# Side work in a routed expert kernel re-spaced: counts one turn behind comparisons, every turn used, a free turn between weight conversions, late pieces from the first network on

## The chip, the cores and the metric

The kernel runs on one core of a Trainium2 chip. Its engines are TensorE (PE, with PEld for the weight loads that overlap it), VectorE (DVE), ScalarE (ACT), GpSimd (POOL) and SyncE (SP, which issues most transfers). The metric is device time in microseconds (us), median of three runs; lower is better.

## The reference, cut to what matters

Three stages follow each other: a gated linear attention over 768 steps, a routed network with eight experts that each take exactly 384 of the 3072 tokens, and one dense network with a cosine in it that every token passes. The routed order is greedy: the logits of all tokens and experts are sorted, and each token goes to the first expert that still has room.

```python
for idx in order:                       # logits, largest first
    tok, e = (int(idx) // E, int(idx) % E)
    if assigned[tok] >= 0 or counts[e] >= cap:
        continue
    assigned[tok] = e
    counts[e] += 1
...
for e in range(E):
    mask = assigned == e
    h = np.maximum(x[mask] @ w1[e], 0.0)
    out[mask] = h @ w2[e]
...
h = x @ w_in
g = h * np.cos(h)
return (g @ w_out).astype(np.float32)
```

Here x has 384 columns, w1 is 384 x 1024, w2 1024 x 384, w_in 384 x 2048 and w_out 2048 x 384. w_in and w_out arrive as 64-bit floats and are brought to 32 bits on the chip.

## The kernel before, in words

Every product is made as three matmuls on a high and a low part of each operand (`mm3`), so one 128 x 384 tile of result with K = 384 costs nine matmuls of 384 columns. The greedy routing is turned into eight rounds: each round fills the expert that saturates first. While the tokens of one expert pass both networks (a stage of `experts`, n = 0 to 7), the routing of the next one runs beside it as side work.

The main work of a stage: a transpose of the gathered tokens (`xpose`, tile xtp, 9 small matmuls), the first network in eight steps `up` (tile pA) and `down` (accB), then the second network in sixteen steps `up2` (pC) and `down2` (accD), where `down2` runs three steps behind `up2`. Each of these is nine matmuls; a piece of nine is called a turn below. `up2` and `finish` also make the cosine: ACT ki (L785), DVE ki (L787), ACT sine (L790), DVE product (L792), ACT gh (L800) and POOL gl (L801); `down2` needs gh and gl.

The side work of a stage is a generator, `beside`. It runs `route` for the next expert, and inside it `search`: six steps k, each of which compares the tokens' best logits with up to 64 thresholds on DVE (tile C, L549, in two halves), counts on PE (tile cn, L545, 12 or 6 small matmuls), forms sat on DVE, sums over thresholds on PE (num, L572) and makes the next thresholds on DVE (thr, L589 or L597). `route` then ranks tokens (rk, L632), compares (L, L661) and inverts the ranks (xi, L658) to the list of tokens (idx). After that `prefetch` gathers those tokens (xg, three indirect transfers that POOL issues) and starts the fetch of weights (raw, from SP), and five calls of `convert` split the weights (ACT wh L723, POOL wl L724).

A second generator, `convert_late`, brings the last six pieces of w_out to 32 bits in stage 0: ACT L137, DVE L139 and L140, DVE L142 and L143, then ACT woh L146 and POOL wol L147; a piece is four calls of `next(late, None)`.

What decides the place of the side work is `tick`, called 42 times in a stage: after each `up` and `down`, and after each `up2` and `down2` but a few. Before the change it advances the side work two times out of three. ACT keeps the written order; PE, DVE and POOL are put in order by a scheduler when the program is built, which keeps close to the written order.

Of the kernel before, what the change touches and what calls it, by code (L numbers as in the profile page):

```python
# [525 lines left out]
def search(nc, K, rp, ps, Z, n, em, found):  # L526
    V, PE = nc.vector, nc.tensor
    mx, oh = Z["mx"], Z["oh"]
    steps = FIRST if n == 0 else LATER
    thr, tau, old = K["t0"].bitcast(F32)[:, ::2 ** (steps[0] - 25)], None, None  # L530
    for k, st in enumerate(steps):
        T = 2 ** ((32 if k == 0 else steps[k - 1]) - st)
        g = P // T if n > 0 else 1
        if st:
            nx = steps[k + 1]
            wd = 2 ** (st - nx)
        if k == 0 and n == 0:
            cn = Z["cn"]
        else:
            C = rp.tile([P, NU, T], BF16, name="C", tag="C")  # L540
            cn = ps.tile([g * T, g * E], F32, name="cn", tag="rt")

            def count(a, z):
                for c in range(a, z, g):
                    PE.matmul(cn, C[:, c:c + g].rearrange("p c t -> p (c t)"), oh[:, c:c + g].rearrange("p c e -> p (c e)"), start=(c == 0), stop=(c == NU - g))  # L545

            cuts = (0, 15, NU) if n == 0 else tuple(range(0, NU + 1, HALF))
            for a, z in zip(cuts, cuts[1:]):
                V.tensor_tensor(C[:, a:z], mx[:, a:z, None].to_broadcast([P, z - a, T]), thr[:, None, :].to_broadcast([P, z - a, T]), op=ALU.is_ge)  # L549
                if n == 0:  # L550
                    count(a, z)
            if n > 0:
                count(0, NU)
            if st and k:
                base = rp.tile([P, wd], I32, name="base", tag="base")
                V.scalar_tensor_tensor(base, K["io"][:, :wd], nx, tau.to_broadcast([P, wd]), op0=ALU.logical_shift_left, op1=ALU.bitwise_xor)
            yield
        sat = rp.tile([T, E], BF16, name="sat", tag="sat")
        if g == 1:
            V.tensor_scalar(sat, cn, CAP - 0.5, None, op0=ALU.is_ge)  # L560
        else:
            less = None
            for j in range(1, g):
                part = cn[j * T:(j + 1) * T, j * E:(j + 1) * E]
                more, less = less, rp.tile([T, E], F32, name="less", tag="less", bufs=2)
                if j == 1:
                    V.tensor_scalar(less, part, -1.0, None, op0=ALU.mult)
                else:
                    V.scalar_tensor_tensor(less, part, -1.0, more, op0=ALU.mult, op1=ALU.add)
            V.scalar_tensor_tensor(sat, cn[:T, :E], 0.5 - CAP, less, op0=ALU.add, op1=ALU.is_ge)  # L570
        num = ps.tile([P, E], F32, name="num", tag="rt")
        PE.matmul(num, K["onesb" if st == 0 else "ones0"][:T], sat, start=True, stop=True)  # L572
        ix = rp.tile([P, 1], I32, name="ix", tag="ix")
        if st == 0:
            top = rp.tile([P, 1], F32, name="top", tag="top")
            V.tensor_reduce(top, num, axis=AX, op=ALU.max)
            sel = rp.tile([P, E], F32, name="sel", tag="sel")
            V.scalar_tensor_tensor(sel, num, top, K["eb"], op0=ALU.is_equal, op1=ALU.mult)
            V.tensor_reduce(em, sel, axis=AX, op=ALU.max)
            V.tensor_scalar(ix, top, -1.0, None, op0=ALU.add)  # L580
            V.tensor_tensor(found, ix, tau, op=ALU.bitwise_xor)
            yield
            break
        with nc.allow_low_precision(reason="small whole numbers"):
            V.tensor_reduce(ix, num, axis=AX, op=ALU.max)
        old, tau = tau, rp.tile([P, 1], I32, name="tau", tag="tau", bufs=2)
        if k:
            thr = rp.tile([P, wd], I32, name="thr", tag="thr", bufs=2)
            V.scalar_tensor_tensor(thr, ix.to_broadcast([P, wd]), st, base, op0=ALU.logical_shift_left, op1=ALU.bitwise_xor)  # L589
            V.scalar_tensor_tensor(tau, ix, st, old, op0=ALU.logical_shift_left, op1=ALU.bitwise_xor)  # L590
        else:
            t2 = rp.tile([P, 1], I32, name="t2", tag="t2i")
            V.tensor_scalar(tau, ix, st, -2**31, op0=ALU.logical_shift_left, op1=ALU.bitwise_xor)
            V.tensor_scalar(t2, tau, 31, 0x7FFFFFFF, op0=ALU.arith_shift_right, op1=ALU.bitwise_and)
            V.tensor_tensor(tau, tau, t2, op=ALU.bitwise_xor)
            thr = rp.tile([P, wd], I32, name="thr", tag="thr", bufs=2)
            V.scalar_tensor_tensor(thr, K["io"][:, :wd], nx, tau.to_broadcast([P, wd]), op0=ALU.logical_shift_left, op1=ALU.bitwise_xor)  # L597
        thr = thr.bitcast(F32)
        yield
    if n == 0:  # L600
        V.tensor_copy(Z["ems"], em)
    else:
        V.tensor_tensor(Z["ems"], Z["ems"], em, op=ALU.add)
# [84 lines left out]
def experts(tc, nc, ctx, K, R, Z, xs, wcat, wout, out):  # L688
# [29 lines left out]
    def convert(r, f, eng=None):  # L718
        if f < NA:
            raw = r["raw"].pop(f)  # L720
            h = mp.tile([P, 2 * HD], F32R, name="wh", tag="wh", bufs=5)
            l = mp.tile([P, 2 * HD], F32R, name="wl", tag="wl", bufs=5)
            SC.copy(h, raw)  # L723
            (eng or GP).tensor_tensor(l, raw, h.bitcast(F32), op=ALU.subtract)  # L724
            r["w"][f] = (h, l)
            fetch(r, f + 3)
# [30 lines left out]
    def up(r, f):  # L757
        p = mmp.tile([P, HD], F32, name="pA", tag="mm")
        wh, wl = r["w"][f]
        for k in range(3):  # L760
            s = slice(k * P, (k + 1) * P)
            mm3(p, (wh[:, s], wl[:, s]), r["xT"][k], k == 0, k == 2)
        r["h"][f] = split(p, "h", 3, "h", relu=True)
# [66 lines left out]
    late = convert_late(nc, mp, R, wout)  # L830
# [17 lines left out]
    with in_order(tc, nc, (mybir.EngineType.Activation,)):  # L848
        for n in range(E):
            r = cur  # L850
            nxt = second if n == 0 else fresh() if n < E - 1 else None

            def beside():
                if nxt is not None:
                    if n == 0:
                        next(steps)
                        hold(tc, nc, mybir.EngineType.DVE, mark)
                        yield
                    yield from steps if n == 0 else route(nc, K, rp, rtp, Z, n + 1, nxt)
                    prefetch(nxt)  # L860
                    yield
                    for f in range(5):
                        convert(nxt, f)
                        yield
            side = beside()
            count = [0]

            def tick():
                count[0] += 1
                if count[0] % 3:  # L870
                    next(side, None)
            for f in range(2, NA):
                up(r, f)
                tick()
                down(r, f - 2)
                convert(r, f + 3)
                tick()
            for d in range(3):
                down(r, NA - 2, (d,))
                down(r, NA - 1, (d,))  # L880
            tick()
            for f in range(LEAD):
                up2(r, f, (0, 1))
            for f in range(LEAD):
                up2(r, f, (2,))
            for f in range(LEAD, LAG):
                up2(r, f)
                next(late, None)
                tick()
                next(late, None)  # L890
            down2(r, (0,))
            tick()
            for f in range(LAG, NF):
                up2(r, f)
                next(late, None)
                tick()
                down2(r, (f - LAG + 1,))
                next(late, None)
                tick()
            for f in range(NF + 1 - LAG, NF - 2):  # L900
                down2(r, (f,))
                tick()
            for _ in side:
                pass
            if nxt is not None:
                xpose(nxt)
                down2(r, (NF - 2,))
                up(nxt, 0)
                up(nxt, 1)
                down2(r, (NF - 1,))  # L910
            else:
                down2(r, (NF - 2, NF - 1))
            cur = nxt
# [95 lines left out]
```

## Time and profile before

| | |
|---|---|
| median of 3 runs | 872.75 us (871.38 to 873.23) |
| profiled execution, its own time | 871.95 us |
| its span, first to last instruction | 870.2 us |
| mean granted TensorE clock | 0.976 |
| stage 0, from its first matmul at 201.13 to 291.74 us | 90.61 us |
| a stage with a search beside it (n = 1 to 5) | 82.73 to 83.26 us |
| the stage with routing but no search (n = 6) | 77.06 us |

The profiled execution lies 1.75 us above its span, and 0.8 us under the median. PE is busy for almost the whole of a stage, so a stage is as long as its matmuls and the holes between them.

### The profile page before, as it was taken

To read this page: it belongs to the slowest core of one execution; us is meant where nothing else is said; L and a number is where in the kernel's file an instruction comes from. 1 tells how busy PE (TensorE), PEld (TensorE's weight loads), DVE (VectorE), ACT (ScalarE), POOL (GpSimd) and SP (SyncE) were. 2 spreads that over 40 slices of the span, in tenths; PEclk is the share of its full clock that TensorE was granted. 3 is DMA by queue.
4 is the path that set the end of the run, shared out by engine and by line. 5 is a ranking of instruction groups with operands and counts; after the bars stand their busy time and mean duration, and the time that the engine had idled before them with its cause. 6 is when DMAs were issued, how large, how long until landed. Compare 5 with 4: busy or idle time off the path is not lost.

```text
span 870.2 us, 15619 instructions
## 1 busy us (share of the span) xinstructions
PE 810.0 (93%) x5886; PEld 760.0 (87%) x5886; DVE 529.8 (61%) x1365; ACT 423.8 (49%) x814; POOL 378.8 (44%) x329
## 2 busy tenths in 40 slices
PE   6989999648998899999999999999999999999996
PEld 4878889527988889999998999899989999999996
DVE  5888888565697368546844683567357645432332
ACT  4777776113355425632563356245624553753552
POOL 5545555013146513751384138314732563734233
PEclk9999999859999999999999999999999999999999
DMA  9988884142032201220131014002300133300000
GB/s 243 262 229 222 232 223 120 40 126 86 1 109 82 83 1 55 72 75 2 55 101 46 1 55 119 28 1 73 101 28 27 60 113 85 92 1 28 1 2 28
DMA packets 27348, 71.91 MB, mean 83 GB/s; under 512 B 4608, under 2 KB 7936, under 8 KB 27264
## 3 DMA queue, kind: packets, MB, share of 16 engines
q1 hardware_dynamic: 24192, 61.38, 24.7%
q0 software_dynamic: 3072, 9.44, 3.4%
q8 instruction: 49, 0.80, 0.4%
q14 instruction: 35, 0.29, 0.1%
HBM read 61.37 MB, written 9.44 MB: 81 GB/s over the span
## 4 chain that ended last, share of the span: by engine, by line
PE 47%; DVE 2%; ACT 1%; issue 0%; POOL 0%; POOLq 0%; ACTq 0%
PE accD L812 5%; PE accD L811 5%; PE accD L813 5%; PE pC L742 5%; PE pC L741 5%; PE pC L743 5%; PE accB L741 2%; PE pA L741 2%; PE accB L742 2%; PE accB L743 2%; PE pA L743 2%; PE pA L742 2%; DVE C L549 1%; DVE thr L597 1%; PE xtp L753 1%; PE cn L545 1%
## 5 line engine op out<-in xcount | busy, mean ns | idle before, releaser
L801 POOL TENSOR_TENSOR gl<-ki,gh 128x384 fp32r<-128x384 f32 x128 | 132.1, 1036 | 249.8 <-ACT gh L800 228.1
L813 PE MATMUL accD<-woh,gl 128*128 128x384 f32 x384 | 131.1, 341 | 5.6 <-POOL gl L801 5.6
L724 POOL TENSOR_TENSOR wl<-raw,wh 128x768 fp32r<-128x768 f32 x61 | 112.7, 1853 | 51.4 <-ACT wh L723 43.5
L811 PE MATMUL accD<-woh,gh 128*128 128x384 f32 x384 | 131.7, 343 | 0.5 <-ACT gh L800 0.5
L812 PE MATMUL accD<-wol,gh 128*128 128x384 f32 x384 | 130.9, 341 | 0.0
L743 PE MATMUL pC<-yTh,wil 128*128 128x384 f32 x384 | 130.3, 339 | 0.0
L741 PE MATMUL pC<-yTh,wih 128*128 128x384 f32 x384 | 130.0, 341 | 0.0
L742 PE MATMUL pC<-yTl,wih 128*128 128x384 f32 x384 | 129.9, 338 | 0.0
L787 DVE SCALAR_TENSOR_TENSOR ki<-pC,ki 128x384 f32<-128x384 f32 x128 | 71.0, 555 | 85.2 <-ACT ki L785 85.0
L785 ACT ACTIVATE ki<-pC,quarter 128x384 int32<-128x384 f32 x128 | 73.7, 576 | 92.2 <-PE pC L743 90.9
L792 DVE TENSOR_TENSOR ki<-pC,ki 128x384 f32<-128x384 f32 x128 | 71.0, 555 | 53.8 <-ACT ki L790 50.3
L790 ACT ACTIVATE ki<-ki,halfpi 128x384 f32<-128x384 f32 x128 | 79.0, 617 | 43.9 <-DVE ki L787 43.6
L732 ACT ACTIVATE hh<-pA 128x384 fp32r<-128x384 f32 x64 | 31.5, 492 | 114.9 <-PE pA L743 114.9
L723 ACT CAST wh<-raw 128x768 fp32r<-128x768 f32 x64 | 52.3, 828 | 61.6 <-PE accB L742 32.2
L813 PEld LDWEIGHTS accD<-woh,gl 128*128 128x128 f32 x384 | 72.7, 189 | 7.3 <-POOL gl L801 7.2
L733 DVE SCALAR_TENSOR_TENSOR hl<-pA,hh 128x384 fp32r<-128x384 f32 x64 | 35.5, 555 | 63.1 <-ACT hh L732 62.9
L811 PEld LDWEIGHTS accD<-woh,gh 128*128 128x128 f32 x384 | 72.8, 189 | 0.9 <-ACT gh L800 0.8
L742 PEld LDWEIGHTS pC<-yTl,wih 128*128 128x128 f32 x384 | 72.5, 189 | 0.6 <-DVE yTl L736 0.5
L800 ACT CAST gh<-ki 128x384 fp32r<-128x384 f32 x128 | 64.8, 506 | 16.8 <-DVE ki L792 16.6
L812 PEld LDWEIGHTS accD<-wol,gh 128*128 128x128 f32 x384 | 72.6, 189 | 0.0
L741 PEld LDWEIGHTS pC<-yTh,wih 128*128 128x128 f32 x384 | 72.5, 189 | 0.1
L743 PEld LDWEIGHTS pC<-yTh,wil 128*128 128x128 f32 x384 | 72.5, 189 | 0.0
(187 smaller groups left out, 1688.8 us busy)
## 6 DMA issues: line engine op xcount, KB each, us to landing
raw<-in_wcat_dram SPq DMA_DIRECT2D x64, 384.0 KB, 3.4
ring<-in_qk_dram SPq DMA_DIRECT2D x48, 192.0 KB, 5.0
vf<-in_qkvf_dram SPq DMA_DIRECT2D x23, 384.0 KB, 4.9
wr<-in_win_dram SPq DMA_DIRECT2D x12, 512.0 KB, 5.4
xs<-xx SPq DMA_DIRECT2D x24, 192.0 KB, 2.7
wr<-in_wout_dram SPq DMA_DIRECT2D x10, 384.0 KB, 4.8
lr<-in_wout_dram SPq DMA_DIRECT2D x6, 384.0 KB, 3.3
vf<-in_qkvf_dram SPq DMA_DIRECT2D x2, 192.0 KB, 3.2
```

Of the source, the lines that this page charges most:

```text
L724: (eng or GP).tensor_tensor(l, raw, h.bitcast(F32), op=ALU.subtract)
L741: PE.matmul(o, ah, bh, start=first, stop=False)
L742: PE.matmul(o, ah, bl, start=False, stop=False)
L743: PE.matmul(o, al, bh, start=False, stop=last)
L785: SC.activation(ki, p, AF.Identity, bias=quarter, scale=INV2PI)
L787: V.scalar_tensor_tensor(fr, p, INV2PI, ki, op0=ALU.mult, op1=ALU.subtract)
L790: SC.activation(fr, fr, AF.Sin, bias=halfpi, scale=TWO_PI)
L792: V.tensor_tensor(g, p, fr, op=ALU.mult)
L801: GP.tensor_tensor(gl, g, gh.bitcast(F32), op=ALU.subtract)
L811: PE.matmul(r["accD"][t], gh[:, s], R["oh"][:, f], start=(f == 0), stop=False)
L812: PE.matmul(r["accD"][t], gh[:, s], R["ol"][:, f], start=False, stop=False)
L813: PE.matmul(r["accD"][t], gl[:, s], R["oh"][:, f], start=False, stop=(f == NF - 1))
```

## The change

It moves the counts of a search (n > 0) one step of the side work behind the comparisons, lets every turn advance the side work, puts an empty step behind each of the five weight conversions, and calls the late pieces twice per step of the first network in stage 0 and once per step of the second (before: only in the second, twice per step).

```diff
@@ -550,6 +550,7 @@
                 if n == 0:
                     count(a, z)
             if n > 0:
+                yield
                 count(0, NU)
             if st and k:
                 base = rp.tile([P, wd], I32, name="base", tag="base")
@@ -862,18 +863,18 @@
                     for f in range(5):
                         convert(nxt, f)
                         yield
+                        yield
             side = beside()
-            count = [0]
 
             def tick():
-                count[0] += 1
-                if count[0] % 3:
-                    next(side, None)
+                next(side, None)
             for f in range(2, NA):
                 up(r, f)
+                next(late, None)
                 tick()
                 down(r, f - 2)
                 convert(r, f + 3)
+                next(late, None)
                 tick()
             for d in range(3):
                 down(r, NA - 2, (d,))
@@ -887,7 +888,6 @@
                 up2(r, f)
                 next(late, None)
                 tick()
-                next(late, None)
             down2(r, (0,))
             tick()
             for f in range(LAG, NF):
@@ -895,7 +895,6 @@
                 next(late, None)
                 tick()
                 down2(r, (f - LAG + 1,))
-                next(late, None)
                 tick()
             for f in range(NF + 1 - LAG, NF - 2):
                 down2(r, (f,))
```

In steps of the side work: a stage with a search had 20 steps of `route`, one of `prefetch` and five of `convert`, spread over turns 1 to 38; it now has 26, 1 and 10, over turns 1 to 37. A comparison and the num of its step stay at the turns where they were (3k + 2 and 3k + 4); the count goes from turn 3k + 2 to 3k + 3. `prefetch` goes from turn 31 to 27, and the conversions from 32, 34, 35, 37, 38 to 28, 30, 32, 34, 36. Stage 0 is one turn ahead of that.

On PE, the second search step of a middle stage (num is the sum of the step before, accB_5760 the first of the three results of `down`, cn the counts). Before:

```order
L743 MATMUL pA<-xTh,wl 128x384
L741 MATMUL accB_5760<-hh,wh 128x384
L742 MATMUL accB_5760<-hl,wh 128x384
L743 MATMUL accB_5760<-hh,wl 128x384
L545 LDWEIGHTS C
L545 MATMUL cn<-oh,C 128x16
```

With the change, a few rows further on in the same `down`:

```order
L742 MATMUL accB_5762<-hh,wh 128x384
L743 MATMUL accB_5762<-hl,wh 128x384
L744 MATMUL accB_5762<-hh,wl 128x384
L545 LDWEIGHTS C
L545 MATMUL cn<-oh,C 128x16
```

The first six counts stood after three of the nine matmuls of `down`, and the other six after four more; now all twelve stand together behind the nine. Third and sixth step, whose six counts stood in two threes, have them together too.

On DVE, the first search step of stage 0 (xTl belongs to the transpose, hl to `up`, lv and lr to the late pieces). Before:

```order
L736 TENSOR_TENSOR xTl<-xtp,xTh 128x384 x3
L549 TENSOR_TENSOR C<-mx,t_118 128x768 x2
L733 SCALAR_TENSOR_TENSOR hl<-pA,hh 128x384 x2
L567 TENSOR_SCALAR less<-cn 64x8
L570 SCALAR_TENSOR_TENSOR sat<-cn,less 64x8
L733 SCALAR_TENSOR_TENSOR hl<-pA,hh 128x384
L585 TENSOR_REDUCE ix<-num 128x1
```

With the change:

```order
L734 SCALAR_TENSOR_TENSOR hl<-pA,hh 128x384 x3
L139 TENSOR_SCALAR lv<-lv 128x384
L140 TENSOR_SCALAR lv<-lv 128x384
L142 SCALAR_TENSOR_TENSOR lv<-lr,lv 128x384
L568 TENSOR_SCALAR less<-cn 64x8
L143 SCALAR_TENSOR_TENSOR lv<-lr,lv 128x384
L571 SCALAR_TENSOR_TENSOR sat<-cn,less 64x8
L586 TENSOR_REDUCE ix<-num 128x1
```

All four operations of a late piece now stand ahead of sat, for which num waits.

On POOL, the end of stage 0 (wl are the conversions, wol the late pieces). Before:

```order
L706 DMA xg<-xs,idx 128x384 x3
L147 TENSOR_TENSOR wol<-lv,woh 128x384
L801 TENSOR_TENSOR gl<-ki,gh 128x384 x2
L147 TENSOR_TENSOR wol<-lv,woh 128x384
L724 TENSOR_TENSOR wl<-raw,wh 128x768
L801 TENSOR_TENSOR gl<-ki,gh 128x384
L724 TENSOR_TENSOR wl<-raw,wh 128x768
L801 TENSOR_TENSOR gl<-ki,gh 128x384
L724 TENSOR_TENSOR wl<-raw,wh 128x768
L147 TENSOR_TENSOR wol<-lv,woh 128x384
L724 TENSOR_TENSOR wl<-raw,wh 128x768
L801 TENSOR_TENSOR gl<-ki,gh 128x384
```

With the change:

```order
L707 DMA xg<-xs,idx 128x384 x2
L802 TENSOR_TENSOR gl<-ki,gh 128x384
L707 DMA xg<-xs,idx 128x384
L147 TENSOR_TENSOR wol<-lv,woh 128x384
L725 TENSOR_TENSOR wl<-raw,wh 128x768
L802 TENSOR_TENSOR gl<-ki,gh 128x384
L725 TENSOR_TENSOR wl<-raw,wh 128x768
L802 TENSOR_TENSOR gl<-ki,gh 128x384
L725 TENSOR_TENSOR wl<-raw,wh 128x768
L802 TENSOR_TENSOR gl<-ki,gh 128x384
L725 TENSOR_TENSOR wl<-raw,wh 128x768
L802 TENSOR_TENSOR gl<-ki,gh 128x384
```

One wl and one gl now alternate, one late piece less stands among them, and the gathers come two gl earlier. In the middle stages the gathers likewise go from behind nine gl to behind seven.

## Rows read from the trace of the kernel before

**Rows 1.** Stages: busy us (x instructions) of each engine, clock, DMA.
```profile
core 0: us, PE busy (x) PEld busy (x) DVE busy (x) ACT busy (x) POOL busy (x), PEclk, DMA share, GB/s
201.13:291.74 90.61, 82.65 (x492) 77.28 (x491) 65.74 (x163) 43.39 (x81) 40.76 (x34) 0.96 0.22 66
...
540.95:623.92 82.97, 81.50 (x513) 77.59 (x511) 50.32 (x140) 38.70 (x71) 36.71 (x31) 1.00 0.17 53
...
706.65:783.71 77.06, 77.06 (x458) 76.44 (x457) 33.35 (x67) 38.55 (x71) 36.88 (x31) 1.00 0.21 62
```

**Rows 2.** What PE waited for in stage 0: us, times, longest.
```profile
PE accD L813 <- POOL gl L801: 5.3, 3, 2.8
PE cn L545 <- DVE C L549: 0.8, 2, 0.6
PE rk L632 <- DVE R L630: 0.6, 1, 0.6
PE accD L811 <- ACT gh L800: 0.5, 1, 0.5
PE xi L658 <- DVE L L661: 0.4, 2, 0.3
PE num L572 <- DVE sat L570: 0.3, 1, 0.3
```

**Rows 3.** The same for the middle stage 540.95 to 623.92.
```profile
PE cn L545 <- DVE C L549: 1.3, 1, 1.3
```

**Rows 4.** Two stretches of the end of stage 0, columns as in Rows 1.
```profile
276.20:279.60 3.40, 3.40 (x12) 3.40 (x12) 3.37 (x4) 0.21 (x1) 2.27 (x2) 0.51 0.52 163
286.90:290.80 3.90, 3.90 (x16) 3.90 (x16) 1.11 (x2) 1.60 (x4) 3.90 (x4) 0.63 0.53 166
```

**Rows 5.** Timeline of PE, that stage's second search step.
```profile
554.11 0.18 PE L572 MATMUL num<-sat,ones 64*128 64x8 bf16 x1
...
557.91 0.31 PE L545 MATMUL cn<-oh,C 128*128 128x16 bf16 x6 [1.32 <-DVE C L549]
...
559.03 0.42 PE L742 MATMUL accB<-hl,wh 128*128 128x384 f32 x1
```

**Rows 6.** Timeline of PE, second search step of stage 0.
```profile
207.84 0.18 PE L572 MATMUL num<-sat,ones 64*128 64x8 bf16 x1
...
211.65 0.31 PE L545 MATMUL cn<-oh,C 128*128 128x16 bf16 x6 [0.29 <-DVE C L549]
212.52 0.31 PE L545 MATMUL cn<-oh,C 128*128 128x16 bf16 x6 [0.56 <-DVE C L549]
212.69 0.43 PE L741 MATMUL pA<-xTh,wh 128*128 128x384 f32 x1
```

**Rows 7.** Timeline of PE around the third and fourth counts, middle stage.
```profile
562.77 0.34 PE L743 MATMUL accB<-hh,wl 128*128 128x384 f32 x1
...
564.21 0.34 PE L742 MATMUL pA<-xTl,wh 128*128 128x384 f32 x1
...
568.39 0.34 PE L743 MATMUL pA<-xTh,wl 128*128 128x384 f32 x1
...
568.99 0.33 PE L742 MATMUL accB<-hl,wh 128*128 128x384 f32 x1
```

**Rows 8.** Timeline of DVE: third step's sat, sixth step's second comparison.
```profile
564.73 0.15 DVE L570 SCALAR_TENSOR_TENSOR sat<-cn,less 32x8 bf16<-32x8 f32 x1
...
583.30 0.54 DVE L549 TENSOR_TENSOR C<-mx,thr 128x384 bf16<-128x384 f32 x1
```

**Rows 9.** Timelines of POOL and DVE, end of stage 0.
```profile
275.45 1.94 POOL L724 TENSOR_TENSOR wl<-raw,wh 128x768 fp32r<-128x768 f32 x1
...
275.74 1.87 DVE L140 TENSOR_SCALAR lv<-lv 128x384 int32<-128x384 int32 x1
```

**Rows 10.** Timeline of POOL, gathers of the middle stage.
```profile
604.80 0.98 POOL L706 DMA_INDIRECT xg<-xs,idx  x1 [1.79 <-DVE idx L675]
606.09 0.96 POOL L706 DMA_INDIRECT xg<-xs,idx  x1 [0.30 <-PE accD L813]
607.07 1.02 POOL L801 TENSOR_TENSOR gl<-ki,gh 128x384 fp32r<-128x384 f32 x1
```

**Rows 11.** Tile thr: duration in ns, least, median, most.
```profile
L597 DVE SCALAR_TENSOR_TENSOR thr<-io,tau x7: 193/1769/1775, 168.1 to 638.1; 128x64 int32<-128x64 int32 x6, 128x32 int32<-128x32 int32 x1
```

**Rows 12.** Timeline of PE, the wait ahead of the first low clock.
```profile
275.55 0.44 PE L813 MATMUL accD<-woh,gl 128*128 128x384 f32 x1 [1.61 <-POOL gl L801]
```

## The prediction

> **What bounds the kernel now.** Read the stages first. In the middle stages PE is busy for 81.5 of 83 us, and a stage whose routing has no search takes 77.06 us [rows 1]; its 458 matmuls stand 0.17 us apart (77.06 / 458), nearly all of them large ones. So the main work sets the time, and all that the change can win is what the side work costs PE: some 6 us in each of the five stages n = 1 to 5, and in stage 0, which takes 90.61 us, more. Then read what PE waits for. In stage 0 the reader is to see waits for gl and gh of 5.3 + 0.5 = 5.8 us, and 0.8 + 0.6 + 0.4 + 0.3 = 2.1 us for the search and the ranks [rows 2]. In a middle stage it is one wait of 1.3 us for a comparison [rows 3]. [...] Last, the timelines show what a count costs where it doesn't wait. The attention and the first search, before 201 us, and the last stage have none of the changed code and stay.
>
> **The middle stages.** No count is added or removed; the gain is in waits and in seams between large and small matmuls.
>
> Second step. From num to the first large matmul behind the counts it takes 559.03 - 554.11 = 4.92 us, with 16 large matmuls in between [rows 5]; the wait is 1.32 us of that. The order puts 18 in between now, as stage 0 has them already: there it takes 212.69 - 207.84 = 4.85 us, and the two halves of the comparison are still waited for, 0.29 and 0.56 us [rows 6]. The comparison starts from the same num, so it ends no earlier, and two large matmuls more ahead of the counts do not cover it. I therefore take stage 0's figure: 4.92 - (4.85 - 2 x 0.17) = 0.4 us. Bounds: 0, and what it would be with no wait left. Stage 0's 4.85 less its two waits and 18 x 0.17 leaves 0.9 us for num and the counts themselves, so that is 4.92 - 16 x 0.17 - 0.9 = 1.3 us.
>
> Third step. Two groups of three counts with five large matmuls take 564.21 - 562.77 = 1.44 us, of which 1.44 - 5 x 0.17 = 0.6 is theirs; six in one group take 568.99 - 568.39 less 2 x 0.17 = 0.26 [rows 7]. Joined: 0.3 us. The sixth step is joined likewise, but its comparison's second half ends at 583.84 [rows 8], about where the joined group now stands, so I take 0.2 of that 0.3.
>
> The new order also shortens something: sat must be ready one turn (nine matmuls, 9 x 0.17 = 1.5 us) behind the count, where it had two. In the third step sat ended at 564.88 [rows 8], 0.7 us behind the start of the second large matmul after its counts, 564.21 [rows 7]; num now stands 8 large ones, 1.4 us, behind that one. So it is covered, if narrowly where an hl of DVE stands in between. The inversion xi comes earlier too; its nearest wait is stage 0's 0.4 us [rows 2], so it costs 0 to 0.4; I take 0, since DVE has no late pieces there.
>
> Sum for a stage: 0.4 + 0.3 + 0.2 = 0.9. Bounds: 0 (the third step's 0.3 against xi's 0.4) and 1.3 + 0.3 + 0.3 = 1.9. Five stages give **4.7** with the decimals kept (0 to 9.5). Stages 6 and 7 have no search; their spacing alone changes, and PE waits for nothing there.
>
> **What moves without a price.** The conversions' ACT and POOL work is the same in number, one wl and one gl for each two turns: 1.9 [rows 9] + 1.0 [rows 10] = 2.9 us of POOL in 3.1 us of PE. The weights' transfers from SP start some four turns earlier, at a DMA share of 0.17 to 0.22 [rows 1]. The gathers go four turns ahead; what they may hold up is a rival below. Without that cover a late wl would hold up the first `up` of the next stage by its own 1.9 us.
>
> **The end of stage 0.** Here conversions, late pieces and gathers meet. What the reader is to see is how DVE and POOL hold each other: L140 took 1.87 us beside a wl of 1.94 [rows 9], and thr of the first search step took 1.77 us in the median against 0.19 at best [rows 11]. [...] The delayed piece stands in DVE's queue ahead of L787, so ki, then gh, then gl are late, and `down2` waits. There were two such chains, and 5.8 us of waits and 3.1 us of low clock came of them: 8.9 us.
>
> [...]
>
> With the change one late piece instead of two runs on DVE beside the conversions, and wl and gl alternate instead of two wl in a row. But POOL starts that stretch behind: three gathers of 1.29 us [rows 10], a wol and a wl in front of it, and the last piece's L139 to L142 stand ahead of a ki. So I expect one chain to stay, with a wait near 2 us and a low clock of half of 3.1: about half of 8.9. Gain **4.9**; bounds 0 (both stay) and 8.9.
>
> **The rest of stage 0.** The waits in [rows 2] for comparison, rank and num (0.8 + 0.6 + 0.3 = 1.7) go, since the two late pieces that stood between num and rk on DVE now stand elsewhere, and stage 0's thr no longer starts beside a wl. The inversion's 0.4 becomes some 1.0 in my estimate: its five groups stand among `down2` and `up2`, and L comes behind a late piece. New is the first network: in the first step L142 and L143 stand ahead of sat, as the order on DVE shows, and one of them meets the wl that starts in that turn, 1.9 us, of which the turn covers little: 1.7 us of wait at num. In the third step the same meets a comparison whose count now stands two turns, 3.1 us, behind num: 0.8, half as much. The third piece has no conversion beside it. Together 1.7 + 0.4 - 1.0 - 1.7 - 0.8 = **-1.4**; bounds -4 (both in full, and the clock falls once, 1.5) and +2.1.
>
> **Sum.** 4.7 + 4.9 - 1.4 = 8.2 us. Against the profiled execution's own 871.95 us that is 863.75; the median lies 0.8 us above it, so 864.5 us.
>
> **Rivals.**
> A, the forecast: 861 to 868 us. Chance 0.60.
> B, every wait goes: 9.5 + 8.9 + 2.1 = 20.5 us, 852.3 us. For it speaks that the counts have a turn more; against it that stage 0's twelve counts have just this distance and wait for 0.85 us [rows 6]. Chance 0.08.
> C, DVE and POOL hold each other in stage 0 as before: the late pieces' operations wait for a wl each in the first network too, and the end keeps both chains; stage 0 gives nothing net and only the 4.7 remains: 868 us. That operations of DVE were held for a whole wl speaks for it [rows 9, 11], the smaller number of pieces in the end against. [...] Chance 0.20.
> D, slower: the gathers. They now stand on POOL ahead of two gl, and the `down2` that needs the first of them starts four turns (4 x 1.53 = 6.1 us) behind the `up2` that makes it. Three gathers of 1.29 us are 3.9, gl itself is 1.0 [rows 10]: 1.2 us of room, in which gh must also be made. They wait for idx, as they did for 1.79 us [rows 10], and hold what stands behind. Each us of idx beyond that room is a us of wait in stages 0 to 5, and a wait above 1.5 us also brings the low clock, 1.5 us (the waits of 1.6 and 2.8 us did, those of 1.3 did not [rows 1, 2, 3, 4, 12]). The gain of 8.2 is used up when gl is 1.4 us late in each of six stages; at 2 us late the loss is 6 x 3.5 = 21, and the time 885 us. Against it: POOL was idle when idx came, and xi is a turn earlier too. Chance 0.06.
> E, no difference: waits move by as much as they shrink (C, with half a us of gather wait per stage), 871 to 874 us. Chance 0.06.
>
> **How the numbers follow.** The time is A's, 864.5. A measurement of this kernel can tell about 0.2%, 1.75 us. A, nearly all of C and B are faster by more: 0.86; E and the rim of C 0.08; D 0.06. The range goes from 858, which leaves out B, to 869.5, which takes in C and leaves out D and E: 0.8.
>
> **What would show it.** In the profile of the changed kernel: the stages n = 1 to 5 at 82 us each, with two short waits for C in the second step and one group of six in the third and sixth; stage 0 at 87 us, with one wait for gl of about 2 us in its end instead of 1.6 and 2.8, and a new wait of num for sat in its first network. Wrong would be: waits for gl in the middle stages (D), a wait for C gone altogether (B), or two low-clock stretches still in stage 0 (C).

## The result, and the profile after

The changed kernel takes 862.86 us (median of 4 runs, 860.03 to 864.1) against 872.34 us before (median of 4, 871.38 to 873.23): a ratio of 0.9885, 95% interval 0.9854 to 0.9916. Forecast were 864.5 us, in a range from 858 to 869.5. The profiled execution has a span of 861.5 us, 8.7 us less than before.

The stages after the change; columns as in [rows 1]:

```profile
201.04:288.56 87.52, 81.74 (x492) 76.44 (x491) 69.62 (x162) 43.35 (x80) 41.31 (x33) 0.97 0.23 66
...
534.14:616.01 81.87, 81.03 (x512) 77.87 (x511) 49.53 (x140) 39.05 (x71) 36.89 (x31) 1.00 0.18 54
...
697.88:774.94 77.06, 77.06 (x459) 76.44 (x457) 33.27 (x67) 38.65 (x71) 36.81 (x31) 1.00 0.19 57
```

Stage 0 went from 90.61 to 87.52 us (3.1 less), the five middle stages from 82.7 to 83.3 each to 81.86 or 81.87 (together from 414.91 to 409.32, 5.6 less); stage 6 is unchanged at 77.06.

What PE waits for in stage 0 now, against [rows 2]: us, times, longest.

```profile
PE accD L814 <- POOL gl L802: 1.7, 1, 1.7
PE num L573 <- DVE sat L571: 1.6, 2, 1.3
PE cn L545 <- DVE C L549: 1.0, 2, 0.7
PE accD L812 <- ACT gh L801: 0.8, 1, 0.8
PE xi L659 <- DVE L L662: 0.4, 1, 0.4
PE rk L633 <- DVE R L631: 0.3, 1, 0.3
```

One wait for gl is left of three, and there is a new one of num for sat. In a middle stage two short waits for C (0.28 and 0.56 us) stand where one of 1.3 us stood [rows 3]. The timeline of PE shows them in the second search step of the stage that [rows 5] came from:

```profile
547.30 0.18 PE L573 MATMUL num<-sat,ones 64*128 64x8 bf16 x1
...
551.11 0.31 PE L545 MATMUL cn<-oh,C 128*128 128x16 bf16 x6 [0.28 <-DVE C L549]
551.98 0.31 PE L545 MATMUL cn<-oh,C 128*128 128x16 bf16 x6 [0.56 <-DVE C L549]
552.14 0.43 PE L742 MATMUL pA<-xTh,wh 128*128 128x384 f32 x1
```

From num to the first large matmul behind the counts it is 552.14 - 547.30 = 4.84 us, with 18 large matmuls between: stage 0's figure of before, 4.85 [rows 6], to 0.01 us.

The new wait in the first network, in the timelines of DVE, POOL and PE: a late piece's L143 starts behind a wl, ends 0.4 us behind it, and sat and num follow.

```profile
208.34 0.56 DVE L142 SCALAR_TENSOR_TENSOR lv<-lr,lv 128x384 int32<-128x384 int32 x1
...
209.02 2.08 DVE L143 SCALAR_TENSOR_TENSOR lv<-lr,lv 128x384 int32<-128x384 int32 x1
211.14 0.16 DVE L571 SCALAR_TENSOR_TENSOR sat<-cn,less 64x8 bf16<-64x8 f32 x1
...
208.87 1.82 POOL L725 TENSOR_TENSOR wl<-raw,wh 128x768 fp32r<-128x768 f32 x1 [8.66 <-ACT wh L724]
...
211.35 0.18 PE L573 MATMUL num<-sat,ones 64*128 64x8 bf16 x1 [1.27 <-DVE sat L571]
```

And the end of stage 0, in the same three timelines:

```profile
261.83 1.50 POOL L707 DMA_INDIRECT xg<-xs,idx  x1 [0.16 <-issue]
263.35 1.02 POOL L147 TENSOR_TENSOR wol<-lv,woh 128x384 fp32r<-128x384 f32 x1
264.34 1.84 POOL L725 TENSOR_TENSOR wl<-raw,wh 128x768 fp32r<-128x768 f32 x1
266.15 1.01 POOL L802 TENSOR_TENSOR gl<-ki,gh 128x384 fp32r<-128x384 f32 x1
...
262.89 4.49 DVE L226 TENSOR_TENSOR w<-w,eb 128x192 f32<-128x192 f32 x1
267.30 0.95 DVE L549 TENSOR_TENSOR C<-mx,t 128x768 bf16<-128x768 f32 x1
268.17 0.55 DVE L788 SCALAR_TENSOR_TENSOR ki<-pC,ki 128x384 f32<-128x384 f32 x1
...
270.65 2.18 DVE L142 SCALAR_TENSOR_TENSOR lv<-lr,lv 128x384 int32<-128x384 int32 x1
272.76 0.55 DVE L788 SCALAR_TENSOR_TENSOR ki<-pC,ki 128x384 f32<-128x384 f32 x1
...
271.46 0.44 PE L812 MATMUL accD<-woh,gh 128*128 128x384 f32 x1 [0.82 <-ACT gh L801]
...
273.75 0.44 PE L814 MATMUL accD<-woh,gl 128*128 128x384 f32 x1 [1.66 <-POOL gl L802]
```

The window right behind it, columns as in [rows 1]:

```profile
274.70:278.00 3.30, 3.30 (x12) 3.30 (x11) 1.48 (x3) 3.08 (x6) 3.24 (x3) 0.52 0.23 54
```

One chain stayed, with a low granted clock behind it once (0.52 over 3.30 us). Its first link is no late piece: L226 is the start of stage 1's search (best_expert), which DVE takes ahead into stage 0. It was held from inside a gather to the end of the gl, through four POOL operations without a gap; the ki behind it was late, then gh. The late piece's L142 came second.

### The profile page after: what moved, and what is told of

It is laid out like the page before. It is cut to its first block, busy times and chain, and to the rows that moved or that the text cites. A ratio compares the mean times of both kernels' runs of the same rounds, so it can differ in the third digit from the quotient of the medians.

```text
span 861.5 us, 15614 instructions
## 1 busy us (share of the span) xinstructions
PE 804.9 (93%) x5884; PEld 759.6 (88%) x5886; DVE 530.0 (62%) x1365; ACT 425.9 (49%) x814; POOL 380.7 (44%) x329
## 4 chain that ended last, share of the span: by engine, by line
PE 67%; DVE 7%; DMA 1%; issue 1%; POOL 1%; ACT 1%; POOLq 0%; SPq 0%; DVEq 0%; ACTq 0%
PE pC L742 7%; PE pC L744 7%; PE accD L812 7%; PE accD L814 7%; PE pC L743 7%; PE accD L813 7%; PE accB L742 4%; PE pA L742 4%; PE pA L743 3%; PE pA L744 3%; PE accB L744 3%; PE accB L743 3%; DVE C L549 2%; DVE thr L598 1%; PE xtp L754 1%
```

## The experiments

Two theories stood against each other at first: that the late pieces cost where they meet a wl and that moving them shortened the end of stage 0; and, as the rival, that the spacing of the conversions did it. Stage 0 is counted in every kernel from its second large matmul (201.13 us before; the first starts 0.36 to 0.46 us earlier). It is split at 262 us: "rest" and "end" are the time by which large matmuls stand further apart than 0.1735 us, added up over the stretch without the transpose, to some 0.2 us. Each ratio is to the kernel before as timed together with that run: 871.13 us for the runs e, 871.89 for f and 871.88 for g.

| kernel | median us | ratio to before, 95% interval | stage 0 | rest | end | stage of n = 1 to 5 |
|---|---|---|---|---|---|---|
| before | 872.34 | | 90.61 | 7.6 | 10.2 | 82.7 to 83.3 |
| changed | 862.86 | 0.9885 (0.9854 to 0.9916) | 87.52 | 10.2 | 4.6 | 81.9 |
| e1_late_as_before | 866.45 | 0.9944 (0.9927 to 0.9961) | 89.26 | 6.8 | 9.8 | 81.9 |
| e2_late_alone | 865.45 | 0.994 (0.9907 to 0.9973) | 84.39 | 10.1 | 1.6 | 82.9 to 83.0 |
| e3_counts_at_once | 868.39 | 0.9961 (0.9944 to 0.9979) | 88.45 | 13.1 | 2.6 | 83.0 |
| e4_no_free_turn | 865.57 | 0.9924 (0.9897 to 0.9951) | 91.40 | 11.2 | 7.6 | 81.9 |
| f1_mixed | 859.61 | 0.9856 (0.9832 to 0.988) | 85.98 | 11.7 | 1.6 | 81.9 |
| f2_mixed_second_later | 861.88 | 0.9888 (0.9868 to 0.9908) | 85.23 | 10.9 | 1.6 | 82.0 |
| f3_late_between | 864.18 | 0.9913 (0.9882 to 0.9945) | 87.34 | 8.1 | 6.5 | 81.9 |
| f4_best_expert_held | 862.06 | 0.9891 (0.9866 to 0.9917) | 84.02 | 9.4 | 1.8 | 83.4, then 81.9 |
| g1_both_apart | 860.39 | 0.9858 (0.9833 to 0.9883) | 83.42 | 8.2 | 2.5 | 82.7, then 81.9 |
| g2_turn_lent | 854.29 | 0.9782 (0.9758 to 0.9807) | 84.35 | 9.1 | 2.6 | 81.5, then 80.7 |

Stage 0 began between 199.0 and 203.5 us in these executions, though no edit touches what stands ahead of it; the stage's own length is free of that. It is not free of the granted clock: e2, f1 and f2 have the same code in stage 0, which took 84.39, 85.98 and 85.23 us with the same end of 1.6; the clock of the stage was 1.00 in e2 and 0.99 in f2, and in f1 it was 0.51 over 6.4 us. So up to 1.6 us of stage 0 between two kernels, each profiled once, need not come from their code. By the whole time, only e1 and e3 (slower) and g2 (faster) have intervals apart from that of the change.

**The late pieces put back.** In the changed kernel the calls return to where they were:

```diff
             for f in range(2, NA):
                 up(r, f)
-                next(late, None)
                 tick()
                 down(r, f - 2)
                 convert(r, f + 3)
-                next(late, None)
                 tick()
...
                 up2(r, f)
                 next(late, None)
                 tick()
+                next(late, None)
...
                 down2(r, (f - LAG + 1,))
+                next(late, None)
                 tick()
```

> The change with the late pieces put back where they were (twice per step of the second network, f = 1 to 12). Nothing of it touches the stages n = 1 to 5: 81.9 us each in both theories. Theory 1 (a late piece costs where it meets a wl: moving them made the end of stage 0 shorter and its first network longer): the wait of num for sat (1.27 us) and the waits for C (0.96 us) in the first network go, the end gets back most of the 5.6 us that it won; stage 0 at 89 to 91 us instead of 87.5, the whole at 864 to 867 us. Rival (the end won by the spacing of the conversions and the earlier gathers alone): the end keeps one chain, the first network's 2.2 us are saved, stage 0 at 85.3 us and the whole at 860.5 us.

Theory 1 gave the figures. The waits for sat and C left the first network, the middle stages did not move, and the end is as costly as before (9.8 against 10.2), with waits for gl of 4.4 us, the longest 2.8. So the even spacing of the conversions alone won next to nothing there.

**The late pieces moved, alone.** In the kernel before:

```diff
                 up(r, f)
+                next(late, None)
                 tick()
                 down(r, f - 2)
                 convert(r, f + 3)
+                next(late, None)
                 tick()
...
                 tick()
-                next(late, None)
             down2(r, (0,))
...
                 down2(r, (f - LAG + 1,))
-                next(late, None)
                 tick()
```

> The kernel before with the late pieces alone moved. Stages n = 1 to 5 stay at 82.7 to 83.3 us. Theory 1: stage 0 gets new waits for sat or C of about 2 us in its first network and loses one of its two low-clock stretches at the end, about 5 us: 87 to 89 us instead of 90.6, the whole at 868 to 870 us. Rival (spacing alone made the end shorter): the end keeps waits for gl of 5 us and two low-clock stretches, the first network's new waits come on top: stage 0 at 92 to 93 us, the whole at 873 to 875 us.

Stage 0 came out better than either theory said, 84.39 us, and better than with the whole change: the spacing takes 3 us back in this execution, and 1.5 and 2.3 against f1 and f2, which have the same stage 0. The window of its stage 0:

```profile
200.97:285.36 84.39, 78.60 (x491) 74.29 (x491) 64.98 (x163) 43.68 (x81) 41.60 (x33) 1.00 0.23 69
```

And its waits of PE:

```profile
PE cn L545 <- DVE C L549: 2.2, 2, 1.1
PE num L572 <- DVE sat L570: 1.7, 2, 1.2
PE rk L632 <- DVE R L630: 0.9, 1, 0.9
PE accD L813 <- POOL gl L801: 0.9, 1, 0.9
```

The cost in the first network is there as expected, the end lost 8.6 us. Against the changed kernel the end is 3.0 us shorter: the waits for gh and gl come to 0.9 instead of 2.5, and the low clock shown above, 0.48 x 3.3 = 1.6 us, did not come. On DVE the search work taken ahead was done by 264.6 us here, and the first wl started at 269.14; in the changed kernel the first wl starts at 264.34, in the middle of it.

**The counts back in the comparison's turn.**

```diff
             if n > 0:
-                yield
                 count(0, NU)
+                yield
```

> The change with the counts of every search put back into the turn of their comparison; num and all other side work stay at their turns. Theory 1 (the stages n = 1 to 5 won 1.1 us each by the later counts alone: 0.43 in the second step, 0.32 in the third, 0.35 in the sixth): these stages go back to 82.9 to 83.0 us, with one wait for C of 1.3 us, and stage 0 changes by less than 1 us; the whole at 867.5 to 869.5 us. Rival (the even spacing of the side work did it): the stages stay near 81.9 us, the whole at 862 to 864 us.

Theory 1: the middle stages return to 82.98 us with the wait of 1.3 us. Their whole gain is the later count. Stage 0 changed by 0.9 us in sum, out of two larger parts. Its rest grew by 2.9 us, with a wait for C of 1.9 and a granted clock of 0.53 over 3.6 us behind it. Its end shrank by 2.0 us, although a comparison of stage 1's search was held there for 7.00 us (266.10 to 273.10), longer than any operation in the other kernels: the waits for gl and gh came to 1.9 and 0.3 us, none above 0.8, and the clock stayed at 1.00. So the length of a hold alone does not set its price.

**No free turn.**

```diff
                         convert(nxt, f)
                         yield
-                        yield
```

> The change without the empty turn behind each conversion: five conversions in five turns. POOL then has 5 x 1.87 + 3 x 1.03 = 12.4 us of work in 5 x 1.53 = 7.7 us, so the last gl comes about 4.7 us late against a room of some 6 us. Theory 1 (that room covers it where DVE has no late piece): stages n = 1 to 5 stay at 81.9 us without a wait for gl, stage 0's end loses 1 to 3 us more; the whole at 863 to 866 us. Rival (the free turn is what keeps gl in time): waits for gl of over 1.5 us and a low clock in every stage, 2 to 4 us each; the whole at 875 to 885 us.

Theory 1 again: the middle stages stay at 81.81 to 81.87 without a wait for gl; the end of stage 0 pays, 3.0 us (waits for gl of 3.8 us, the longest 3.0). The other 0.9 us of stage 0 is in its rest, where the first matmuls stood 0.32 us apart for longer in this execution: 12 such gaps, against 5 in the change, at a granted clock of 0.56 there.

**Stage 0 and the other stages each by what suited them.** The counts are later for n > 1, the free turn is there for n > 0, and in stage 0 two turns of three are used:

```diff
-            if n > 0:
+            if n > 1:
                 yield
+            if n > 0:
                 count(0, NU)
...
                         convert(nxt, f)
                         yield
-                        yield
+                        if n > 0:
+                            yield
...
             def tick():
-                next(side, None)
+                turns[0] += 1
+                if n > 0 or turns[0] % 3:
+                    next(side, None)
```

> Stage 0 as in the kernel before with the late pieces alone moved (two turns of three used, counts at once, no free turn), stages n = 1 and later as in the changed kernel. Theory 2 (in stage 0 the moved late pieces gain and the even spacing loses, because it starts the conversions beside the search work of stage 1 that DVE does ahead; in the other stages the later counts gain): stage 0 at 84.4 us with a clock of 1.00, stages 1 to 5 at 81.9 us, the whole at 859 to 861 us, 2 to 3 us under the changed kernel. Rival (the 84.4 us were one lucky meeting of operations): stage 0 at 86 to 89 us, the whole at 862 to 865 us.

859.61 in all and 81.9 us for the stages 1 to 5, as theory 2 had it, and the end of stage 0 as short as in e2 (1.6 us). Stage 0 as a whole took 85.98 us, not 84.4, and so ended at the lower edge of the rival's range: the granted clock was 0.51 over 6.4 us of its first network (last section).

**The second step's counts a further turn later.** In the mixed kernel:

```diff
             if n > 1:
                 yield
+                if k == 1:
+                    yield
             if n > 0:
                 count(0, NU)
```

> The mixed kernel, with the twelve counts of the second search step (where PE waits for C twice, 0.28 + 0.56 us) one turn later still, and num and all that follows one turn later with them, in the stages n = 1 to 5. Theory 2: both waits go and the twelve counts join, 1.48 us become 0.32: 1.2 us for each of five stages, which come to 80.7 us; the whole at 853 to 855 us. Rival (the turn is missing at the other end: the last conversion stands at turn 37 of 42 and its wl or the gathers come late): the wait for C goes, but waits of up or of xpose, or for gl, take its place, the stages stay at 81.5 us or more and the whole at 858 us or more.

The rival's side of the bound, by another way than it named. The second step's 1.48 us became 0.32, but all later steps moved by a turn against the networks, and the sixth step's six counts split in threes and waited, as PE's timeline shows:

```profile
332.62 0.24 PE L545 MATMUL cn<-oh,C 128*128 128x32 bf16 x3 [0.62 <-DVE C L549]
```

**The late pieces between the two groups of conversions.** In the changed kernel:

```diff
                 up(r, f)
-                next(late, None)
+                if f > 5:
+                    next(late, None)
                 tick()
                 down(r, f - 2)
                 convert(r, f + 3)
-                next(late, None)
+                if f > 5:
+                    next(late, None)
                 tick()
...
+            next(late, None)
             tick()
...
                 up2(r, f)
                 next(late, None)
+                next(late, None)
                 tick()
             down2(r, (0,))
+            next(late, None)
+            next(late, None)
             tick()
...
                 down2(r, (f - LAG + 1,))
+                next(late, None)
                 tick()
```

> The changed kernel with the late pieces between the two groups of conversions of stage 0: one call a turn from turn 9, two in turns 14 to 17, one to turn 28. All six pieces are done, with nearly the same DVE work in the first network as to number of pieces a turn, but beside no wl. Theory 1 (only the meeting with a wl costs): the late piece's operations take 0.35 to 0.56 us each but for meetings with a wol or gl of 1.0 us, the waits for sat of 1.27 and for C of 0.96 us go, and at the end the piece whose L142 took 2.18 us is gone, with it the wait for gl of 1.66 us and the low clock: stage 0 at 83.5 to 85.5 us, the whole at 859 to 861 us. Rival (the pieces cost as such, by standing ahead of the search on DVE): waits for sat, C, R or L of 2 us and more in the second network take their place, stage 0 at 87 to 88 us.

The first half held: no wait for sat or C in the first network, whose rest fell to 8.1 us in spite of a wait of 1.4 us for L. The second half failed: without a late piece beside them the end stayed at 6.5 us. There the comparison C of stage 1's search, which takes 0.94 us, was held through a whole run of POOL; PE then waited 1.5 us for the gh behind it, and the clock was 0.59 over the next 4 us. The timelines of DVE and POOL show the hold:

```profile
265.17 6.59 DVE L549 TENSOR_TENSOR C<-mx,t 128x768 bf16<-128x768 f32 x1
271.69 0.55 DVE L793 TENSOR_TENSOR ki<-pC,ki 128x384 f32<-128x384 f32 x1
...
265.37 1.88 POOL L725 TENSOR_TENSOR wl<-raw,wh 128x768 fp32r<-128x768 f32 x1
267.18 1.01 POOL L802 TENSOR_TENSOR gl<-ki,gh 128x384 fp32r<-128x384 f32 x1
268.13 1.01 POOL L147 TENSOR_TENSOR wol<-lv,woh 128x384 fp32r<-128x384 f32 x1
269.11 1.84 POOL L725 TENSOR_TENSOR wl<-raw,wh 128x768 fp32r<-128x768 f32 x1
```

**Stage 1's search not taken ahead.**

```diff
-                    yield from steps if n == 0 else route(nc, K, rp, rtp, Z, n + 1, nxt)
+                    own = steps if n == 0 else route(nc, K, rp, rtp, Z, n + 1, nxt)
+                    if n == 1:
+                        so_far = {i.name for i in nc.cur_bb.bb.instructions}
+                        next(own)
+                        hold(tc, nc, mybir.EngineType.DVE, so_far)
+                        yield
+                    yield from own
```

> The changed kernel, where DVE may not take the first work of stage 1's search (best_expert, L221 to L228, and the first comparison C) ahead into the end of stage 0. There L226 took 4.49 us beside a gather, a wol and a wl of POOL that followed each other. Theory 2 (that held L226 is the first link of the chain behind the waits for gh of 0.82 and gl of 1.66 us): the chain starts 4 us later or not at all, the wait for gh goes and that for gl falls below 1 us, the clock stays at 1.00 behind it; stage 0 at 83.5 to 85.5 us, stage 1 within 0.3 us of 81.9. Rival (the late piece's L142, held for 2.18 us by a wl, is enough): a wait for gl of 1 to 2 us stays, stage 0 at 86 to 87.5 us.

Theory 2's time for stage 0 (84.02 us, clock 1.00), with a wait for gl of 1.2 us left, as the rival had it: now L139 of the late piece was held, for 5.93 us. The work held back was then late for the first count of stage 1 (a wait of 2.49 us), and that stage took 83.4 us. By the whole time this kernel can't be told from the change (0.9891 against 0.9885).

**Both kept away.** The edit of f3_late_between, and that of f4_best_expert_held with an earlier mark, so that the search work stands right behind the last ki of stage 0:

```diff
+                    if n == 1:
+                        next(own)
+                        hold(tc, nc, mybir.EngineType.DVE, mark)
+                        yield
...
             for _ in side:
                 pass
+            if n == 0:
+                mark = {i.name for i in nc.cur_bb.bb.instructions}
```

> The changed kernel with both kinds of movable DVE work kept away from the conversions of stage 0: the late pieces between the two groups of conversions (one call a turn from turn 9, two in turns 14 to 17, one to turn 28), and the first work of stage 1's search (best_expert and its first comparison) behind the last ki of stage 0. Theory 3 (any DVE operation on SBUF that meets a run of POOL operations is held for the whole run, 4.5 us for L226 in the changed kernel, 5.9 us for L139 and 6.6 us for C in the two runs that kept only one of the two away; the ki behind it, then gh and gl, are late): no wait for gh and none over 0.5 us for gl at the end of stage 0, the clock 1.00 there; the two runs' figures give 87.3 - 6.2 = 81 us for stage 0 and 81.9 for stage 1, the whole at 856 to 858 us. Rival (POOL itself is late, with gathers, five wl and a gl each two turns): waits for gl of 1 us and more stay without any held operation, stage 0 at 83 us or more, the whole at 859 us or more.

The expected time was missed, in stage 0 too (83.42 us against 81). Nothing on DVE was held in that stretch any more and the clock stayed at 1.00, but three waits for gl remain, as the rival had it, though none above 0.8 us. POOL itself is late there, as its timeline shows: three gathers and a gl in front of the first wl.

```profile
259.62 0.96 POOL L707 DMA_INDIRECT xg<-xs,idx  x1 [0.46 <-ACT gh L801]
260.88 1.00 POOL L707 DMA_INDIRECT xg<-xs,idx  x1 [0.30 <-issue]
261.90 1.00 POOL L802 TENSOR_TENSOR gl<-ki,gh 128x384 fp32r<-128x384 f32 x1
...
264.05 1.86 POOL L725 TENSOR_TENSOR wl<-raw,wh 128x768 fp32r<-128x768 f32 x1
```

Its waits for gl in stage 0:

```profile
PE accD L814 <- POOL gl L802: 1.7, 3, 0.8
```

Stage 1 took 82.7 us: the first count no longer waits, but `up` waits 0.6 us for the xTl behind the search work. So nothing is won over the mixed kernel (860.39 against 859.61, intervals that overlap).

**A turn lent by the first step to the second.** To the kernel above:

```diff
             if n > 0:
-                yield
+                if n == 1 or k > 0:
+                    yield
+                if n > 1 and k == 1:
+                    yield
                 count(0, NU)
```

> The kernel g1_both_apart, with one turn lent from the first search step to the second in the stages n = 1 to 5: the first step's count stands in its comparison's turn again (that comparison is made long ahead), the second step's count two turns behind its comparison; everything from its num on stays at its turn. Theory 3: the second step's waits for C (0.28 + 0.56 us) and its split go, 1.48 us become 0.32, and nothing else changes: 80.7 us for each of the five stages against 81.9, the whole 5 to 6 us under the other. Rival (what the second step wins comes back as a wait elsewhere, as when all that follows moved a turn): the stages stay at 81.5 us or more, the whole within 2 us of the other.

Theory 3, to the tenth in four of the five stages; stage 1, which began from 82.7, fell by as much, to 81.5. The windows of stage 0 and of a middle stage:

```profile
200.93:285.28 84.35, 80.08 (x492) 74.96 (x491) 60.71 (x159) 43.10 (x80) 40.54 (x33) 0.99 0.23 69
...
528.22:608.92 80.70, 80.70 (x512) 77.80 (x511) 48.09 (x140) 39.04 (x71) 37.17 (x31) 1.00 0.18 55
```

PE is busy for the whole of the middle stage. At 854.29 us this kernel beats both: 0.9782 of the time before, against 0.9885 for the change, with intervals apart.

## Why the prediction was right, and where not

**The middle stages (4.7 us).** Right: 5.6 us, and all of it from the later counts (e3). In the stage shown it is 0.43 for the second step (forecast 0.4), 0.32 for the third (0.3), 0.35 for the sixth, where 0.2 was taken because its comparison ended about where the counts now stand; they didn't wait there. That is the term which was too small. That C would still be waited for, and the size of the waits, came from stage 0's own rows, the nearest there were. Sat and xi cost nothing, as taken.

**The end of stage 0 (4.9 us).** The size was near, 10.24 - 4.57 = 5.67 us, and one chain with one low clock stayed. The 4.9 does not follow from the figures beside it: a wait of 2 us and a low clock of 1.55 leave 5.35 of the 8.9 us as gain, and half of 8.9 is 4.45. The 3.1 us of low clock in the 8.9 is an estimate, 0.49 x 3.4 + 0.37 x 3.9, from the granted clocks of 0.51 and 0.63 in [rows 4]. Of the two reasons given one was right: moving the late pieces did it. The other, that wl and gl alternate, did not: with the late pieces in place the spacing wins 0.5 us there (e1), and with them moved it loses 3 (changed kernel against e2). The step that failed is "the delayed piece stands in DVE's queue": the longest delay is on best_expert and C, which DVE takes ahead, and which the new spacing brings beside the first conversions. Nor did L226 take about the time of one POOL operation, as L140 did in [rows 9]: it took 4.49 us, where the longest one beside it took 1.84. With the search work held back the end was 2.8 us shorter (f4), some 1.6 of it the low clock that did not come; the hold of 7.00 us in e3 went with an end of 2.6 us, so where the hold falls counts as well as its length, and that part of the account rests on one execution of each kernel. The free turn is worth 3.0 us there (e4).

**The rest of stage 0 (-1.4 us).** It is -2.64: 10.25 against 7.61 us. The named costs came, and near their size in the first network: the wait of num for sat behind L143 measured 1.27 (1.7), those for C in the third step 0.96 (0.8); xi took 0.4 (1.0). Too hopeful was that the last num's wait and the ranks' would go: 0.35 and 0.3 us stayed. And 0.8 us is a low clock at the first matmuls of the stage, ahead of all changed code (0.56 over 1.96 us); e1, f3 and f4, which share that code, did not have it (1.00 in f4), so it is none of the change's. Some 0.7 us remain that no wait in the list shows.

Together 5.59 + 5.67 - 2.64 = 8.6 of the 8.7 us of the span; 8.2 were forecast, and the terms' errors mostly cancel.

**The rivals.** B fell: C is still waited for. C fell, since stage 0 gave 3.1 us net, but its mechanism is what the first network shows: L143, which began 0.15 us after a wl of 1.82 us (209.02 against 208.87), took 2.08 us, against 0.54 at its shortest in the same trace. D fell in the middle stages, which have no wait for gl or gh; of its mechanism g1 shows a trace in stage 0 (0.8 us). E fell with the time.

## What to carry to other kernels

Look at what a moved operation of DVE will stand beside on POOL, the work that a scheduler takes ahead included: one and the same move of the late pieces was worth 4.6 to 6.2 us of stage 0 in the old spacing (e2, f1 and f2 against before) and 1.7 in the new. A consumer put one turn later won what its wait and its split had cost, and no more (1.1 us a stage with the change, 1.2 more in g2); find the turn to lend where the producer is done long ahead, so that the rest of the order stays where it is.

## What was not expected of the hardware

Some DVE operations that work on SBUF alone were held not for one POOL operation but until a run of them had ended. L226 (0.34 us when free) took 4.49, L139 5.93, C 6.59 us, each ending 0.2 to 0.8 us behind the last of a run of POOL operations that followed each other within 0.03 us. It is not so at every meeting. L142 of the changed kernel (270.65 to 272.83) was let through behind a wl, although a gl followed at once, as POOL's timeline shows:

```profile
270.61 1.81 POOL L725 TENSOR_TENSOR wl<-raw,wh 128x768 fp32r<-128x768 f32 x1 [3.45 <-ACT wh L724]
272.38 1.31 POOL L802 TENSOR_TENSOR gl<-ki,gh 128x384 fp32r<-128x384 f32 x1
```

In the twelve traces 30 DVE operations took at least 0.3 us more than at their shortest and began inside a POOL operation that another followed within 0.06 us. 13 of them were held through two to five POOL operations; 11 of these began inside a gather and two inside a wol. The other 17, begun inside a wl, a gl or a wol, were let through behind that one operation. What decides between the two stays open. The operations of DVE that read PSUM for ki (ki<-pC) took 0.53 to 0.56 us everywhere, beside POOL operations or not.

The clock did not follow from the length of a wait. The mixed kernel (f1) and the one with the late pieces alone (e2) have the same code in stage 0 and the same two waits for C (1.13 and 1.03 us), after which the granted clock was 0.51 in the one and 1.00 in the other; f2, again with that code and waits of 1.14 and 1.02, had 1.00. Behind a wait of 2.49 us in f4 it was 1.00. The window behind those waits in f1_mixed:

```profile
213.00:219.40 6.40, 6.40 (x26) 5.95 (x27) 3.75 (x13) 1.76 (x3) 1.80 (x2) 0.51 0.02 4
```

The same in e2_late_alone:

```profile
214.90:219.40 4.50, 4.50 (x35) 4.07 (x36) 3.58 (x12) 1.85 (x4) 1.73 (x2) 1.00 0.02 4
```

And behind the wait of 2.49 us in f4_best_expert_held:

```profile
301.40:304.40 3.00, 3.00 (x25) 2.73 (x22) 2.01 (x9) 0.49 (x1) 0.00 (x0) 1.00 0.00 0
```

And one wait of 1.61 us for gl brought 0.51 in the kernel before [rows 4, 12], while another of the same length, at the end of stage 0 in e1_late_as_before, did not:

```profile
287.65 0.44 PE L814 MATMUL accD<-woh,gl 128*128 128x384 f32 x1 [1.61 <-POOL gl L802]
...
287.90:290.50 2.60, 2.60 (x16) 2.60 (x16) 1.59 (x3) 1.77 (x5) 1.69 (x2) 1.00 0.40 136
```

So the prediction's price of the low clock for every wait above 1.5 us (in D) was not a rule, and why the clock fell behind one wait and not behind the other stays open.
